# A linear-attention and gated feed-forward kernel: new load order, batch 0 reordered, attention of batch 2 moved into H1

## The chip, the cores and the metric

The kernel runs on one core of a Trainium2 chip. The metric is the device time of one execution in microseconds (us), here the median of several runs; a profile of one execution shows where its time goes. The engines are PE (TensorE, the matrix products; PEld is its weight load), DVE (VectorE), ACT (ScalarE), POOL (GpSimd) and SP (SyncE, which here only issues DMAs).

## The reference

Inputs q, k, v have 8 batches of 8 heads, 576 rows and 64 columns, in f32. The output has 4608 rows of 512.

```python
def phi(x):
    return np.where(x > 0, x, np.exp(x) - 1.0) + 1.0
q_p, k_p = (phi(q), phi(k))
kv = np.einsum('bhsd,bhse->bhde', k_p, v)
z = np.sum(k_p, axis=2)
num = np.einsum('bhsd,bhde->bhse', q_p, kv)
den = np.einsum('bhsd,bhd->bhs', q_p, z)[..., None] + 1e-06
attn = num / den                        # x: rows of 8 heads x 64 = 512
h = x @ w_in                            # 512 -> 2048
g = h * (1.0 / (1.0 + np.exp(-beta * h)))
y = g @ w_out                           # 2048 -> 512
```

## The kernel before

Each batch has two halves. The attention makes phi(q) and phi(k) in bf16 (ACT's exp, DVE's relu and min: `phi_part`, `phi_relu`, `phi_min`, lines 133 to 153), the products k'v with a column of ones that gives the sums of k (`kv_products`, `kv_both`, lines 169 to 192), the transposes of phi(q) (`q_trans` on PE, or `q_trans_dma`, a DMA transpose from SP), five blocks of numerators with a denominator, a reciprocal and a product on DVE each (`numer`, line 229), and the transposes of the result into `xT` (`x_trans` on PE, `x_trans_dma` from SP). The feed-forward part has an H phase, 16 groups `ff` of four products of 512 columns each with a silu on ACT, and a Y phase, four row blocks of 16 products, evicted by DVE and stored by SP in two DMAs each (`y_out`, line 307). The 576 rows of a batch are 512 plus 64; the eight remainders of 64 make a ninth feed-forward pass at the end, the tail.

The order is written out by hand (`tc.manual_schedule()`): each engine executes its instructions in the order of the program text, and SP and POOL are also the queues that DMAs are issued from. The order is:

- Loads (lines 90 to 111). Eight heads lie as four per half of the partitions, so `load` issues two DMAs of 64 partitions for each tensor (line 80). POOL issues the loads that turn f32 into bf16: half of k, half of q and v of batch 0, w_in in four parts, k and q of batch 1. SP issues the other halves of k and q of batch 0 in f32 (`k0f`, `q0f`), beta, later w_out and v.
- Batch 0 (lines 341 to 404): ten warm products, beta, phi k, six warm products, phi q, copies of v into `vaug`, k'v, the five numerators and transposes interleaved with the first four `ff`, then the rest of H0. w_out and v of batch 1 are issued from SP in it, k and q of batch 2 from POOL (line 405). DVE multiplies half of w_out by 1/beta, POOL the other half (`w_out_scale`).
- Y0 (lines 410 to 442): three quarters of the y products, then the attention of batch 1 between the last quarter's.
- H1 and Y1 (lines 475 to 492): H1 has loads and copies of v beside it; Y1 has the attention of batch 2, with transposes on PE.
- From batch 2 on (line 495) H of batch b holds the numerators of batch b+1 and Y its phi of batch b+2, with transposes by DMA.

PSUM has four banks for h and y (`mmps`), two for the numerators (one buffer, `numps`) and two for transposes and k'v (`miscps`). Output goes through three rotating `y_sb` buffers; e and r of phi have three each.

Of the kernel before, what the change touches and what calls it, by code (L numbers as in the profile page):

```python
# [16 lines left out]
def kernel(  # L17
# [21 lines left out]
    EA = D + 1  # L39
    TINY = 2.0 ** -30  # L40

# [3 lines left out]
    mmps = ctx.enter_context(tc.tile_pool(name="mmps", bufs=4, space=bass.MemoryType.PSUM))  # L45
    numps = ctx.enter_context(tc.tile_pool(name="numps", bufs=1, space=bass.MemoryType.PSUM))
    miscps = ctx.enter_context(tc.tile_pool(name="miscps", bufs=2, space=bass.MemoryType.PSUM))
    work = ctx.enter_context(tc.tile_pool(name="work", bufs=2))


    NX = 3
    xk = [consts.tile([P, 4, J, D], BF16, name=f"xk{i}") for i in range(NX)]
    xq = [consts.tile([P, 4, J, D], BF16, name=f"xq{i}") for i in range(NX)]
    vf = [consts.tile([P, 4, J, D], F32, name=f"vf{i}") for i in range(2)]
# [3 lines left out]
    xT = [consts.tile([P, KC, 512], BF16, name=f"xT{i}") for i in range(3)]  # L58
# [3 lines left out]
    warm = consts.tile([P, 512], BF16, name="warm")  # L62

# [5 lines left out]
    k0f = stage[:, 0:1152].rearrange("p (h j d) -> p h j d", h=2, j=J)  # L69
    q0f = stage[:, 1152:2304].rearrange("p (h j d) -> p h j d", h=2, j=J)  # L70
    v0b = vf[0].rearrange("p h j d -> p (h j d)").bitcast(BF16)[:, 0:2304].rearrange(
        "p (h j d) -> p h j d", h=4, j=J
    )

    def heads(src, b, hh, h0, n):
        return src[b, hh * 4 + h0 : hh * 4 + h0 + n].rearrange(
            "h (g j) d -> g h (j d)", j=J
        )

    def load(eng, dst, src, b, h0=0, n=4):  # L80
        return [
            eng.dma_start(  # L82
                out=dst[hh * G : (hh + 1) * G].rearrange("p h j d -> p h (j d)"),
                in_=heads(src, b, hh, h0, n),
            )
            for hh in range(2)
        ]
# [3 lines left out]
    load(nc.gpsimd, xk[0][:, 0:2], k, 0, 0, 2)  # L91
    load(nc.sync, k0f, k, 0, 2, 2)
    load(nc.gpsimd, xq[0][:, 0:2], q, 0, 0, 2)
    load(nc.sync, q0f, q, 0, 2, 2)
    beta_row = consts.tile([FC, P], F32)
    nc.sync.dma_start(out=beta_row, in_=moe_beta.rearrange("(c p) -> c p", p=P))
    load(nc.gpsimd, v0b[:, 0:2], v, 0, 0, 2)
# [8 lines left out]
    w_in_dma = [  # L106
        nc.gpsimd.dma_start(out=w_in_sb[i], in_=w_in_v[:, :, i * 512 : (i + 1) * 512])
        for i in range(4)
    ]
    load(nc.gpsimd, xk[1], k, 1)  # L110
    load(nc.gpsimd, xq[1], q, 1)

    def load_w_out(i, after=None):
        d = nc.sync.dma_start(out=w_out_f[i], in_=w_out_v[:, i * 4 : (i + 1) * 4, :])
        if after is not None:
            tc.add_manual_dep(d.ins, after.ins.name, SYNC, reason="share of the queues")
# [4 lines left out]
    nc.vector.memset(kvmask[D:P, :, 1, :], 1.0)  # L121
    for i in range(2):
        nc.vector.memset(vaug[i][:, :, :, :, D : D + 2], 1.0)

    def idle(n, cols=512):
        for _ in range(n):
            wp = mmps.tile([P, 512], F32, tag="mm", name="warm_ps")
            nc.tensor.matmul(wp[:, 0:cols], warm[:, 0:P], warm[:, 0:cols], start=True, stop=True)
# [4 lines left out]
    def phi_part(b, a, pr, x):  # L133

        e = work.tile([P, 2, J, D], BF16, tag="e", name="e", bufs=3)
        nc.scalar.activation(e, x, ACTF.Exp)  # L136
        st[b, a, pr, "e"] = e

    def phi_relu(b, a, pr, x):
        r = work.tile([P, 2, J, D], BF16, tag="r", name="r", bufs=3)  # L140
        nc.vector.tensor_scalar(r, x, 0.0, 1.0, ALU.max, ALU.add)  # L141
        st[b, a, pr, "r"] = r

    def phi_tile(b, a):
        st[b, a] = work.tile([P, 2, J, P], BF16, tag=f"phi{a}", name=f"phi_{a}")
# [9 lines left out]
    def xin(b, a, pr):  # L155
        if b == 0:
            if pr == 1:
                return k0f if a == "k" else q0f
            return (xk if a == "k" else xq)[0][:, 0:2]
        return (xk if a == "k" else xq)[b % NX][:, 2 * pr : 2 * pr + 2]  # L160

    def v_copy(eng, b, pr):
        src = v0b if b == 0 else vf[b % 2]
        eng.tensor_copy(  # L164
            vaug[b % 2][:, pr, :, :, 0:D],
            src[:, 2 * pr : 2 * pr + 2].rearrange("p h j d -> p j h d"),
        )

    def kv_products(b, prs, ps):
        for pr in prs:  # L170
            for j in range(J):
                for hh in range(2):
                    r = slice(hh * G, (hh + 1) * G)
                    nc.tensor.matmul(  # L174
                        ps[hh, pr],
                        st[b, "k"][r, pr, j, :],
                        vaug[b % 2][r, pr, j, :, 0:EA],
                        start=(j == 0), stop=(j == J - 1), skip_group_check=True,
                    )

    def kv_tile(b):
        st[b, "kv"] = work.tile([P, 2, 2, 2 * EA], BF16, tag="kv_bd", name="kv_bd")

    def kv_both(b):

        t = [miscps.tile([P, 2, 2 * EA], F32, tag="misc", name="kvp") for _ in range(2)]
        kv_products(b, (0, 1), {(hh, pr): t[hh][:, pr] for hh in range(2) for pr in range(2)})
        kv_tile(b)
        for hh in range(2):
            nc.vector.tensor_mul(  # L190
                st[b, "kv"][:, hh], t[hh], kvmask.rearrange("p a g e -> p a (g e)")
            )

    def q_trans(b, t, eng):

        js = [j for j in (2 * t, 2 * t + 1) if j < J]
        if t == 0:
            st[b, "qT"] = work.tile([P, NT, 2, 2, P], BF16, tag="qT", name="qT")
        tp = miscps.tile([P, 2, 2, 2, G], BF16, tag="misc", name="qtp")
        for pr in range(2):  # L200
            for i, j in enumerate(js):
                nc.tensor.matmul(  # L202
                    tp[:, pr, :, i, :], st[b, "q"][:, pr, j, :], identity,
                    is_transpose=True, start=True, stop=True, skip_group_check=True,
                )
        n = len(js) * G
        dst = st[b, "qT"][:, t, :, :, 0:n].rearrange("p a h n -> p (a h) n")
        src = tp.rearrange("p a h i g -> p (a h) (i g)")[:, :, 0:n]
# [4 lines left out]

    def q_trans_dma(b):
        st[b, "qTd"] = work.tile([P, 2, 2 * J, G], BF16, tag="qT", name="qTd")
        for hh in range(2):
            nc.sync.dma_start_transpose(
                out=st[b, "qTd"][:, hh],
                in_=st[b, "q"][hh * G : (hh + 1) * G].rearrange("p a j c -> p (a j c)"),
            )  # L220

    def q_stat(b, t, hh, pr, n):
# [4 lines left out]
        return st[b, "qT"][:, t, pr, hh, 0:n]  # L227

    def numer(b, t):
        n = P if t < NT - 1 else G  # L230
        nps = numps.tile([P, 2, 512], F32, tag="num", name="nps")
        for hh in range(2):
# [11 lines left out]
        xs = work.tile([P, 2, 4, D], BF16, tag="xs", name="xs", bufs=4)  # L244
        nc.vector.tensor_mul(  # L245
            xs[:n], nv[:, :, :, 0:D], rden[:n, :, :, None].to_broadcast([n, 2, 4, D])
        )
        st[b, "xs", t] = xs

    def x_dst(b, t):  # L250
        if t < NT - 1:
            return xT[b % 3][:, :, t * P : (t + 1) * P]
        return xT_tail[:, :, b * G : (b + 1) * G]

    def x_trans(b, t, eng):
        n = P if t < NT - 1 else G
        xv = st[b, "xs", t].rearrange("p a h d -> p (a h d)")
        tp = miscps.tile([P, KC, P], BF16, tag="misc", name="xtp")
        for p in range(KC):
            nc.tensor.matmul(  # L260
                tp[:, p, :n], xv[:n, p * P : (p + 1) * P], identity[:n, :n],
                is_transpose=True, start=True, stop=True, skip_group_check=True,
            )
        if eng is nc.scalar:
            nc.scalar.copy(x_dst(b, t), tp[:, :, :n])
        else:
            eng.tensor_copy(x_dst(b, t), tp[:, :, :n])

    def x_trans_dma(b, t):
        n = P if t < NT - 1 else G  # L270
        nc.sync.dma_start_transpose(
            out=x_dst(b, t),
            in_=st[b, "xs", t][:n].rearrange("p a h d -> p (a h d)"),
        )


    def h_mm(b, x, ff, hp, c0=0, c1=512):
# [13 lines left out]
    def mm_tile(name):  # L291
        return mmps.tile([P, 512], F32, tag="mm", name=name)

# [10 lines left out]
    def rows(b, j):  # L304
        return out[b * S : (b + 1) * S, :].rearrange("(g j) m -> j g m", j=J)[j]

    def y_out(b, t, yp, c0=0, c1=512, eng=None):
        y_sb = work.tile([P, DM], F32, tag="y_sb", name="y_sb", bufs=3)
        (eng or nc.vector).tensor_copy(y_sb[:, c0:c1], yp[:, c0:c1])  # L309
        for i in range(2):  # L310
            dst = rows(b, 2 * t + i) if b < B else rows(2 * t + i, J - 1)
            nc.sync.dma_start(out=dst[:, c0:c1], in_=y_sb[i * G : (i + 1) * G, c0:c1])

    def w_out_scale(eng, i):
        for c in range(4):
# [3 lines left out]
                None, ALU.mult,  # L319
            )  # L320

    def load_kq(b):
        if b < B:
            load(nc.gpsimd, xk[b % NX], k, b)
            load(nc.gpsimd, xq[b % NX], q, b)

    def load_v(b):
        if b < B:
            load(nc.sync, vf[b % 2], v, b)

    def phi_all(b, a):
        phi_tile(b, a)
        for pr in range(2):
            phi_part(b, a, pr, xin(b, a, pr))
        for pr in range(2):
            phi_relu(b, a, pr, xin(b, a, pr))
        for pr in range(2):
            phi_min(b, a, pr)


    idle(10)
    bps = miscps.tile([P, FC], F32, tag="misc", name="bps")
# [202 lines left out]
```

## Time and profile before

| | us |
|---|---|
| median of 3 runs (325.47 to 330.0) | 328.07 |
| the profiled execution, first to last instruction | 328.0 |
| busy: PE, ACT, DVE, POOL | 295.7, 160.2, 119.4, 55.6 |
| mean granted PE clock | 0.951 |

The profiled execution gives its span, first to last instruction; no other time of its own is listed for it. The page also divides the span into 40 slices (a digit is the busy share in tenths), and the trace gives, for any stretch, the busy time of each engine, the granted clock of PE (1.00 or 0.50) and what the DMAs moved, and for each instruction how long its engine was idle before it and what ended that. Waits and shares are inferred from semaphore events. Batches from the third on repeat with a period of 30.3 us.

### The profile page before, as it was taken

The numbers are of one execution on the slowest core, as the hardware profiler recorded it, in microseconds if no ns is written. First come the engines' busy times: TensorE is split into PE (matmuls) and PEld (weight loads), VectorE is DVE, ScalarE is ACT, GpSimd is POOL, SyncE is SP. The second block draws the span as 40 slices with busy tenths as digits, with TensorE's granted clock in tenths as the row PEclk, the third lists the DMA queues.
The fourth block names the chain that finished last, engine by engine and source line by source line (L and its number), as shares of the span: only waits on it lengthen the run. The fifth ranks groups of instructions, "written<-read, shape, count | busy, mean of one in ns | idle before, by whom it ended". The sixth has DMA issues, their size and how long they took to land.

```text
span 328.0 us, 4511 instructions
## 1 busy us (share of the span) xinstructions
PE 295.7 (90%) x1739; PEld 144.9 (44%) x1767; DVE 119.4 (36%) x272; ACT 160.2 (49%) x208; POOL 55.6 (17%) x70
## 2 busy tenths in 40 slices
PE   5377899786999499999999999999999999999994
PEld 1145544532455244445444544554454444444443
DVE  1564606351048905532551436154425110010011
ACT  0612885362692247816682585378256018306600
POOL 8520067940220004102300200020000000000000
PEclk9565999997899979999999999999999999999999
DMA  7999998299519187987988525942723140041032
GB/s 171 210 207 280 286 273 208 37 187 211 132 26 189 27 155 143 174 146 196 129 132 191 141 43 82 199 113 28 152 50 64 40 88 10 0 97 33 0 66 65
DMA packets 47510, 40.82 MB, mean 124 GB/s; under 512 B 26352, under 2 KB 36864, under 8 KB 47488
## 3 DMA queue, kind: packets, MB, share of 16 engines
q1 hardware_dynamic: 36608, 28.99, 40.3%
q0 software_dynamic: 10880, 11.54, 22.5%
q8 instruction: 14, 0.23, 0.3%
q14 instruction: 8, 0.07, 0.1%
HBM read 36.71 MB, written 9.44 MB: 141 GB/s over the span
## 4 chain that ended last, share of the span: by engine, by line
PE 82%; DVE 7%; DMA 4%; issue 3%; ACT 2%; SPq 1%; DVEq 0%
PE h_ps L279 38%; PE y_ps L297 36%; PE nps L234 4%; PE kvp L174 3%; DMA beta_row<-in_moe_beta_dram 2%; DVE xs L245 2%; DMA out_dram<-y_sb 2%; DVE y_sb L309 1%; PE qtp L202 1%; SPq L82 1%; DVE rden L243 1%; ACT qT L210 1%; DVE r L141 1%; DVE phi_q L148 1%; PE xtp L260 1%
## 5 line engine op out<-in xcount | busy, mean ns | idle before, releaser
L287 ACT ACTIVATE g<-h_ps,beta_c 128x512 bf16<-128x512 f32 x144 | 98.2, 687 | 105.5 <-PE h_ps L279 103.3
L279 PE MATMUL h_ps<-xT,w_in 128*128 128x512 bf16 (+1 forms) x513 | 122.8, 386 | 8.5 <-DVE y_sb L309 3.5
L297 PE MATMUL y_ps<-w_out,g 128*128 128x512 bf16 (+2 forms) x580 | 127.2, 374 | 1.3 <-DVE y_sb L309 0.6
L279 PEld LDWEIGHTS <-w_in 128*128 128x128 bf16 x592 | 57.5, 100 | 71.7 <-issue 13.9
L297 PEld LDWEIGHTS <-g 128*128 128x128 bf16 x592 | 57.0, 98 | 64.9 <-issue 0.8
L309 DVE COPY y_sb<-y_ps 128x512 f32<-128x512 f32 (+2 forms) x37 | 24.8, 673 | 88.0 <-PE y_ps L297 82.2
L164 POOL CAST vaug<-vf 128x1152 bf16<-128x1152 f32 x14 | 16.6, 1214 | 123.2 <-DMA vf<-in_v_dram 98.1
L245 DVE TENSOR_TENSOR xs<-nps,rden 128x512 bf16<-128x512 f32 (+1 forms) x40 | 27.6, 690 | 1.4
L148 DVE TENSOR_TENSOR phi_k<-e,r 128x1152 bf16<-128x1152 bf16 x16 | 12.1, 787 | 25.6 <-ACT e L136 25.6
L136 ACT ACTIVATE e<-xk 128x1152 bf16<-128x1152 bf16 x15 | 16.7, 1151 | 7.5 <-DVE phi_q L148 7.4
L242 DVE TENSOR_SCALAR den<-nps 128x8 f32<-128x8 f32 (+1 forms) x40 | 6.5, 164 | 32.0 <-PE nps L234 32.0
L148 DVE TENSOR_TENSOR phi_q<-e,r 128x1152 bf16<-128x1152 bf16 x16 | 11.8, 753 | 13.9 <-ACT e L136 13.9
L136 ACT ACTIVATE e<-xq 128x1152 bf16<-128x1152 bf16 x15 | 16.5, 1151 | 0.0
L317 POOL TENSOR_SCALAR w_out<-stage,rbeta 128x512 bf16<-128x512 f32 x8 | 12.6, 1591 | 20.8 <-DMA stage<-in_moe_w_out_dram 20.8
L190 DVE TENSOR_TENSOR kv_bd<-kvp,kvmask 128x260 bf16<-128x260 f32 x14 | 5.3, 423 | 26.9 <-PE kvp L174 26.9
L279 PE MATMUL h_ps<-xT_tail,w_in 128*128 128x512 bf16 x63 | 13.9, 379 | 0.1
L136 ACT ACT_TABLE_LOAD x7 | 9.0, 1283 | 8.9 <-DMA xk<-in_k_dram 8.8
L82 POOL DMA_DIRECT2D xk<-in_k_dram x16 | 10.2, 645 | 9.7 <-ACT e L136 5.3
L174 PE MATMUL kvp<-vaug,phi_k 64*128 64x130 bf16 x288 | 10.9, 229 | 0.4 <-ACT qT L210 0.3
L82 POOL DMA_DIRECT2D xq<-in_q_dram x16 | 10.4, 663 | 4.5 <-DMA w_in<-in_moe_w_in_dram 3.8
L174 PEld LDWEIGHTS <-phi_k 64*128 64x128 bf16 x288 | 9.3, 100 | 4.1 <-issue 2.6
L234 PEld LDWEIGHTS <-qTd 128*128 128x128 bf16 (+1 forms) x100 | 7.5, 100 | 6.8 <-DVE xs L245 2.1
(46 smaller groups left out, 116.1 us busy)
## 6 DMA issues: line engine op xcount, KB each, us to landing
out_dram<-y_sb SPq DMA_DIRECT2D x70, 128.0 KB, 2.4
vf<-in_v_dram SPq DMA_DIRECT2D x14, 576.0 KB, 7.3
xk<-in_k_dram POOLq DMA_DIRECT2D x14, 288.0 KB, 6.6
xq<-in_q_dram POOLq DMA_DIRECT2D x14, 288.0 KB, 9.6
w_in<-in_moe_w_in_dram POOLq DMA_DIRECT2D x4, 512.0 KB, 10.6
g<-in_moe_w_out_dram SPq DMA_DIRECT2D x2, 1024.0 KB, 13.1
stage<-in_moe_w_out_dram SPq DMA_DIRECT2D x2, 1024.0 KB, 22.5
stage<-in_k_dram SPq DMA_DIRECT2D x2, 288.0 KB, 4.3
```

What stands on the lines that cost most here:

```text
L82: eng.dma_start(out=dst[hh * G : (hh + 1) * G].rearrange("p h j d -> p h (j d)"), in_=heads(src, b, hh, h0, n),)
L136: nc.scalar.activation(e, x, ACTF.Exp)
L148: nc.vector.tensor_tensor(st[b, a][:, pr].rearrange("p j (h d) -> p j h d", h=2), st[b, a, pr, "e"].rearrange("p h j d -> p j h d"), st[b, ...
L164: eng.tensor_copy(vaug[b % 2][:, pr, :, :, 0:D], src[:, 2 * pr : 2 * pr + 2].rearrange("p h j d -> p j h d"),)
L174: nc.tensor.matmul(ps[hh, pr], st[b, "k"][r, pr, j, :], vaug[b % 2][r, pr, j, :, 0:EA], start=(j == 0), stop=(j == J - 1), skip_group_chec ...
L234: nc.tensor.matmul(nps[:n, hh, pr * 2 * EA : (pr + 1) * 2 * EA], q_stat(b, t, hh, pr, n), st[b, "kv"][:, hh, pr, :], start=True, stop=True ...
L245: nc.vector.tensor_mul(xs[:n], nv[:, :, :, 0:D], rden[:n, :, :, None].to_broadcast([n, 2, 4, D]))
L279: nc.tensor.matmul(hp[:, c0:c1], w_in_sb[ff // 4][:, kc, (ff % 4) * P : (ff % 4 + 1) * P], x[:, kc, c0:c1], start=(kc == 0), stop=(kc == K ...
L287: nc.scalar.activation(g_sb[b % 2][:, ff, :], hp, ACTF.Silu, scale=beta_c[:, ff : ff + 1])
L297: nc.tensor.matmul(yp[:, c0:c1], g_sb[b % 2][:, ff, t * P : (t + 1) * P], w_out_sb[i][:, c, c0:c1], start=(ff == 0), stop=(ff == FC - 1), ...
L309: (eng or nc.vector).tensor_copy(y_sb[:, c0:c1], yp[:, c0:c1])
L317: eng.tensor_scalar(w_out_sb[i][:, c, :], w_out_f[i][:, c, :], rbeta[:, ff : ff + 1], None, ALU.mult,)
```

## The change

- Loads: head 2i+a takes the partition half a, so one DMA of 128 partitions brings a tensor. SP issues only the first half of q and beta. All else goes on POOL in the order q, k, v of batch 0, w_in, half of w_out, k, q, v of batch 1, the other half of w_out, k and q of batch 2, and so on. k and q have two buffers instead of three, v one.
- Batch 0: a dummy exp at the start, q before k, one product column for the sums of k and a set of 20 two-column products for all denominators ahead of the second half of v, then the numerators without denominators; the first four `ff` in passes of 128 columns.
- PSUM: four single banks and two pairs; k'v, numerators and transposes share the pairs. Transposes of q go 1024 columns at a time.
- Y0: the third quarter of y moves behind the attention products; the first y block is evicted by ACT, the exps of batch 2 start there. Two tiles with four fixed slots replace `y_sb`. `w_out_scale` multiplies by 1/beta and by 1.0.
- H1 holds the numerators of batch 2, as later H phases do for theirs; Y1 becomes like the later Y phases. e and r of phi have two buffers, phi q and phi k one.
- `FAST` is empty: `y_fast`, `w_sums`, `g_diff` and `g_sums` issue nothing.

The core of the diff:

```diff
+    q0f = stage[:, 2048:3200].rearrange("p (i j d) -> p i j d", i=2, j=J)
+    def load(eng, dst, src, b, i0=0, n=4):
+        return eng.dma_start(
+            out=dst.rearrange("p i j d -> p i (j d)"),
+            in_=src[b].rearrange("(i a) (g j) d -> (a g) i (j d)", a=2, j=J)[:, i0 : i0 + n],
         )
-    load(nc.gpsimd, xk[0][:, 0:2], k, 0, 0, 2)
-    load(nc.sync, k0f, k, 0, 2, 2)
-    load(nc.gpsimd, xq[0][:, 0:2], q, 0, 0, 2)
-    load(nc.sync, q0f, q, 0, 2, 2)
+    nc.scalar.activation(act0, warm[:, 0:1], ACTF.Exp)
+    load(nc.sync, q0f, q, 0, 0, 2)
...
+    load(nc.gpsimd, xq[0][:, 2:4], q, 0, 2, 2)
+    load(nc.gpsimd, xk[0][:, 0:2], k, 0, 0, 2)
+    load(nc.gpsimd, xk[0][:, 2:4], k, 0, 2, 2)
     load(nc.gpsimd, v0b[:, 0:2], v, 0, 0, 2)
     load(nc.gpsimd, v0b[:, 2:4], v, 0, 2, 2)
...
+    def load_w_out(i):
+        nc.gpsimd.dma_start(out=w_out_f[i], in_=w_out_v[:, i * 4 : (i + 1) * 4, :])
+    load_w_out(0)
+    load_w_out(1)
     load(nc.gpsimd, xk[1], k, 1)
     load(nc.gpsimd, xq[1], q, 1)
...
+    idle(6)
...
+    phi_part(0, "q", 0)
+    phi_part(0, "q", 1)
+    q_trans(0, (0,), (nc.vector,))
+    phi_part(0, "k", 0)
+    q_trans(0, (1,), (nc.scalar,), nc.vector)
+    phi_part(0, "k", 1)
+    for pr in range(2):
+        for j in range(J):
+            for hh in range(2):
+                nc.tensor.matmul(
+                    zps[:, hh, pr : pr + 1], st[0, "k"][half(hh), pr, j, :], ones[half(hh)],
...
+    kv_first(0)
+    for t in range(NT):
+        n = rows_of(t)
+        for hh in range(2):
+            for pr in range(2):
+                nc.tensor.matmul(
+                    dps[:n, t, hh, pr], st[0, "qT"][:, pr, t, hh, 0:n], zbd[:, hh, pr, :],
...
+    idle(3)
+    kv_first(1)
+    for t in range(4):
+        numer_first(t, bank("nps0", [P, 2, 2, P]))
...
+    for t in range(4):
+        x_trans(0, t, nc.scalar, xtp0[:, t % 2, t // 2])
+        if t:
+            for ff in range(4):
+                h_mm(xT[0], ff, hp0[ff], (t - 1) * P, t * P)
...
+    load_v(1)
     load_w_out(2)
-    load_v(1)
     load_w_out(3)
+    load_kq(2)
...
+    for pr in range(2):
+        v_copy(nc.gpsimd, 1, pr)
+    load_v(2)
+    for i in range(2):
         for t in range(4):
             y_mm(0, t, i, yps[t])
+    w_out_scale(nc.gpsimd, 2)
     w_out_scale(nc.gpsimd, 3)
+    q_trans(1, (0, 1), (nc.scalar, nc.vector), nc.vector)
     kv_both(1)
+    for t in range(2):
+        y_mm(0, t, 2, yps[t])
     numer(1, 0)
...
+    y_out(0, 0, yps[0], eng=nc.scalar)
+    phi_exp(2, "k", 0, xin(2, "k", 0))
     y_mm(0, 2, 3, yps[2])
+    x_trans(1, 4, nc.vector)
+    y_out(0, 1, yps[1])
+    phi_exp(2, "k", 1, xin(2, "k", 1))
     y_mm(0, 3, 3, yps[3])
+    y_out(0, 2, yps[2])
+    y_out(0, 3, yps[3])
+    for pr in range(2):
+        phi_relu(2, "k", pr, xin(2, "k", pr))
+        phi_min(2, "k", pr)
+    for pr in range(2):
+        phi_part(2, "q", pr)
+    load_kq(3)
...
+    for b in range(1, B + 1):
+        n, m = b + 1, b + 2
...
+            if n == 2:
+                at(sh, 0, lambda: q_trans_dma(2))
+                at(sh, 0, lambda: [v_copy(nc.gpsimd, 2, pr) for pr in range(2)], lambda: load_v(3))
             at(sh, 3, lambda: kv_both(n))
             for t in range(NT):
-                at(sh, 5 + 2 * t, lambda t=t: numer(n, t))
-                at(sh, 6 + 2 * t, lambda t=t: x_trans_dma(n, t))
+                at(sh, (6, 8, 9, 10, 12)[t], lambda t=t: numer(n, t))
+                at(sh, (6, 8, 9, 10, 12)[t], lambda t=t: x_trans_dma(n, t))
+        if m < B:
+            at(sy, y(0, 0), lambda: phi_tile(m, "q"), lambda: phi_part(m, "q", 0))
+            at(sy, y(1, 0), lambda: phi_part(m, "q", 1))
+            at(sy, y(3, 2), lambda: q_trans_dma(m))
+            at(sy, y(6, 2), lambda: phi_all(m, "k"))
+            at(sy, y(6, 4), lambda: [v_copy(nc.gpsimd, m, pr) for pr in range(2)])
+            at(sy, y(7, 5), lambda: load_kq(m + 1), lambda: load_v(m + 1))
```

Here `y(a, f)` gives `a`. `phi_part` of the new kernel is exp, relu and min of one half; `kv_first` is 18 products of k'v without the column of ones, and one product with the mask; `numer_first` is four products and one product on DVE with the reciprocals made earlier.

## The prediction

> **What bounds the kernel now.** I read the page's 40 slices first, then the busy time by stage, then the timeline around every place where TensorE (PE) idles, then the clock by 3.4 us stretches. The slices:
>
> ```profile
> PE   5377899786999499999999999999999999999994
> PEclk9565999997899979999999999999999999999999
> ```
>
> From slice 15 (115 us) on PE is full at full clock; before that it is neither. By stage (stretch, length, busy time and count of PE, PEld, DVE, ACT, POOL, granted clock, DMA share, GB/s):
>
> ```profile
> 0.00:36.80 36.80, 22.17 (x147) 12.74 (x148) 17.14 (x46) 11.77 (x16) 13.86 (x28) 0.72 1.09 224
> 36.80:47.20 10.40, 10.32 (x48) 4.70 (x49) 2.41 (x6) 8.99 (x14) 3.12 (x3) 1.00 1.11 277
> 47.20:70.50 23.30, 19.90 (x157) 10.45 (x157) 11.77 (x25) 11.40 (x17) 19.71 (x18) 1.00 0.75 150
> 70.50:90.60 20.10, 16.73 (x62) 6.92 (x65) 2.59 (x5) 11.55 (x17) 2.23 (x2) 0.83 0.81 169
> 90.60:114.60 24.00, 19.16 (x157) 10.52 (x158) 18.95 (x45) 11.96 (x12) 2.60 (x4) 1.00 0.44 83
> 114.60:146.70 32.10, 31.71 (x181) 15.11 (x185) 12.45 (x29) 17.89 (x22) 4.95 (x6) 0.95 0.90 154
> 146.70:177.00 30.30, 30.14 (x183) 14.59 (x184) 12.95 (x29) 17.88 (x22) 4.63 (x6) 1.00 0.91 154
> ```
>
> The rows are: start, rest of H0, Y0 with attention of batch 1, H1, Y1 with attention of batch 2, then whole batches. A batch in the steady state is 30.3 us with PE busy for 30.1: nothing is left there without fewer products. Y alone is 64 products of 512 columns, 64 x 0.216 = 13.8 us (the chain has 7.12 + 6.64), so H with attention is 16.5. The early stages hold what can be had: Y1 takes 24.0 instead of 13.8, H1 20.1, the next batch 32.1 instead of 30.3, and the start. Where PE stands there (start, us, engine, line, operation, idle before it and who ended it):
>
> ```profile
> 8.80 1.28 ACT L136 ACT_TABLE_LOAD   x1 [8.80 <-DMA xk<-in_k_dram]
> ...
> 44.08 6.19 POOL L317 TENSOR_SCALAR w_out<-stage,rbeta 128x512 bf16<-128x512 f32 x4 [19.18 <-DMA stage<-in_moe_w_out_dram]
> ...
> 77.51 0.69 DVE L309 COPY y_sb<-y_ps 128x512 f32<-128x512 f32 x1 [5.85 <-DMA out_dram<-y_sb]
> ...
> 78.25 12.54 PE L279 MATMUL h_ps<-xT,w_in 128*128 128x512 bf16 x43 [3.24 <-DVE y_sb L309]
> ```
>
> The first exp waits for k and then for a table load; at 77.5 DVE waits for an output DMA to give a y_sb buffer back, and PE with it. That stall is paid twice, as the clock shows:
>
> ```profile
> 19.30:22.70 3.40, 3.40 (x41) 2.19 (x40) 1.87 (x5) 0.00 (x0) 1.17 (x2) 0.50 1.24 206
> 22.70:26.10 3.40, 1.65 (x22) 1.17 (x20) 1.72 (x7) 1.40 (x4) 0.61 (x1) 1.00 1.19 230
> ...
> 73.90:77.30 3.40, 1.11 (x6) 0.39 (x4) 0.00 (x0) 1.49 (x3) 0.00 (x0) 1.00 1.14 245
> 77.30:80.70 3.40, 2.45 (x6) 0.84 (x6) 1.43 (x3) 0.55 (x1) 0.00 (x0) 0.50 0.86 226
> 80.70:84.10 3.40, 3.40 (x9) 1.18 (x8) 0.00 (x0) 1.36 (x3) 0.00 (x0) 0.50 0.89 188
> ```
>
> A stretch in which PE is full is followed by clock 1.00, one in which it is half idle or more by 0.50; the two half-clock stretches after the stall cost 3.4 us.
>
> **The change, stage by stage.** The sum is made against the profiled span, 328.0 us; the median of the three runs is 328.07, so I take them as the same.
>
> *Start to the end of H0 (47.2 before).* Loads: the first half of q goes alone on SP (one call for two); k's first half on SP took 4.3 us to land from issues at 0.73 and 1.56, so q lands at about 6.1. The other five half tensors go on POOL's queue at 206 GB/s of landed bytes (0.295 MB in 1.4 us each): q 7.5, k 8.4 and 9.8, v 11.3 and 12.7, then w_in 2.5 each, the last at 23. The dummy exp takes the 1.28 us table load off the path, so the first exp runs at 6.1 instead of 10.1. Then ACT and DVE alternate: exp 1.15, relu 0.4 to 0.95, min 0.75, one 1024-wide copy of qT on each engine (twice 0.42, twice 0.58, wider than any row). Both phis are done at about 14.0; before, the last min ended at 17.95. After that PE is in order. Sums of k: of 36 one-column products, 18 lie behind the last min; the kvp products at half clock took 2.06 for 36, so 1.0 (to 15.1, two small copies beside). kv first half 1.0 (16.1). Twenty two-column denominator products: no row; between 0.03 each (kvp, full clock, 1.16 for 36) and 0.155 (nps at half clock, 0.62 for 4), I take 0.10, nps at full clock: 2.0 (18.1). Three warm products 0.43 each: 1.3 (19.4). kv second half 1.0 or, at full clock, 0.6 and its mask product 0.49: 20.9. Numerator 0.4, xs 0.69 (den and reciprocal are gone from here: 5 x 0.37 saved), transposes 0.4, copy 0.58: first h at 23.2. Four passes of 16 products of 128 columns: 0.11 at half clock, 0.055 at full, with transposes 0.4 each and a short wait for the last xs: 5.8, half of it at half clock, to 29.0. Before, this point was 36.8. Twelve h groups of 0.866 follow: H0 ends at 39.4, **-7.8**. Ends: dps and h all at full clock 36.5; all at half clock and loads 1 us later 43.
>
> *Y0 with attention of batch 1 (23.3 before).* 32 y products 6.9 (46.3). ACT reaches table load and four exps after the last silu (40.3 + 1.3 + 4.6 = 46.2), min q 47.0, transposes to 47.8, copies on ACT then DVE (1.05 + 0.8, in series by the order's waits), kv 1.2: 50.2. Then eight y groups of 0.866 and, between them, five numerators (0.42) and transposes (0.4): 11.0, to 61.2. So 21.8: **-1.5**. POOL must keep up: the w_out loads and v now follow in its queue, and no f32 load on POOL is in the trace. Bounds: the 206 GB/s of its casting loads, and SP's w_out rate, 281 GB/s with peaks over 400 between 47 and 52. I take 350, since the bytes and the tile shape are SP's: w_out0 26, w_out1 29, k 32, q 35, v 38.5, w_out2 and 3 by 42 and 45. Then POOL: casts of v 3.1 (41.6), scaling 6.2 and 6.4 as before (48.5, 55), needed at 50.2 and 55.9. It fits, by 1 us. The second multiplication in the scaling has no POOL row; on DVE the two-op relu costs 0.65 ns an element against 0.9 for the one-op scaling, so zero; the upper end is double, 12.6 more in all.
>
> *H1 with attention of batch 2.* PE work as in the steady state, 16.5. Four separate y slots instead of three rotating ones remove the 5.85 us DMA wait. What is late next: DVE must copy y (0.9), do both phi k (2 x 1.15) after Y0; with two e buffers instead of three, exp q waits for these mins, its second ends 4.4 after Y0, the table load 1.28 comes behind it, and the first silu ends at 6.4. PE has four PSUM banks and kv until then, 4.65: **wait 1.8**. Then phi q ends at 5.5, the two DMA transposes of q take 1.9 of SP each and land 4.4 after issue (SP rows of qTd), so at 11.8; PE wants the first numerator at 9.0: **wait 2.8**. Queued behind them on SP are the xT transposes, which have a whole Y of room. Half clock after these waits: none to 3.4, partly absorbed by the second wait; I take 0.9. H1 22.0 against 20.1: **+1.9**, between -3.6 (no wait) and +6.
>
> *Y1*: 13.8 against 24.0: **-10.2**. *Batch 2*: no half clock, 30.3 against 32.1: **-1.8**. *The rest* (181.3): same products. The numerators at slots 8, 9, 10 come every 1.1 us and DVE needs 1.06 for each; two PSUM buffers cover that. v, k and q loads are issued in Y, half a batch ahead, though v has one buffer now: 0.
>
> Sum: 328.0 - 7.8 - 1.5 + 1.9 - 10.2 - 1.8 = 308.6, say **309**.
>
> **Weighed against the Trainium skill.** POOL's 36 load issues took 0.61 to 0.77 us each, among them four at 12.4 to 15.0 with DVE in relu and min, so I charge the moved issues nothing. The page "SBUF — State Buffer", section "SBUF: two separate sides", speaks against the move: while DVE runs a two-port operation, GpSimd cannot write descriptors, and an issue of 620 ns becomes 3100. By that, the eleven w_out and v issues moved from SP could cost up to 2.5 us each of POOL time, an estimate of 27 us, some 10 of them ahead of Y0's scaling, and the sum would be about 319.
>
> **Rivals.**
> 1. POOL becomes the bound of Y0. For: 19.7 of 23.3 us busy there already, 1 us of slack by my count. At 206 GB/s for f32, 5.1 us for each w_out and 5.7 for v, w_out3 lands 10 us later and scaling ends at 62.5, 6.6 after PE's need: 315. With a doubled scaling cost alone it ends at 67: 320; with both, at 75: 328.
> 2. The start gains only half: the chain to the first h is the same length in instructions, and its PE work sits at half clock, as 9.0 to 22.7 and 26.1 to 32.9 before. H0 ends at 43: 313.
> 3. H1 has no waits (exps early enough): 303.
> 4. Slower: the single load queue starves the steady state. One v buffer and 2.4 MB landing through POOL per batch; q of the next batch would hold PE. Against: loads have from the middle of Y to the end of the next H, 22 us, and need 9 to 10. It decides when a batch's loads take over 22 us: to lose 19 us, six batches must each lose 3.2, so loads of 25 us; for +2% 26.3. At 30 us a load: 309 + 6 x 8 = 357.
> 5. The change doesn't do what it says: the q-first order gains nothing because all queues share the DMA engines. The order alone puts q ahead, so only part: this is inside rival 2.
>
> **How the numbers follow.** Forecast 309 (range of its own 304 to 314) 0.60; rival 1 0.13; rival 2 0.10; rival 3 0.08; rival 4 0.04; a mixture of 1 and 2, or both halves of 1, 322 to 328, 0.05. The range 302 to 320 leaves out rival 4, the mixture and a tail of rival 3: under 2 in 10. About 2% (321.5 and 334.6) is what a measurement of this kernel can tell from no change: faster 0.91, same 0.05 (the mixture), slower 0.04.
>
> **What would show it.** First exp near 6; first h near 23 and the last of H0 near 39.4; POOL's last w_out scaling ending before PE asks for it (about 55); H1 starting near 61 with two PE waits, one on ACT's silu, one on a DMA of qTd; Y1 of 13.8 and batches of 30.3. I am wrong if PE waits for POOL in Y0, if batches exceed 30.5, or if the clock stays at 0.5 through H0.

## The result: slower, and the profile after

The changed kernel takes 337.97 us (median of 4 runs, 337.09 to 339.54) beside 328.72 us (325.47 to 330.0) for the kernel before on the same chip: a ratio of 1.029, 95% interval 1.023 to 1.035. The forecast was 309. The profiled execution took 338.02 us, with a span of 336.1.

From the page, the slices of PE and of its granted clock:

```profile
PE   4487997971999899969999399999999999999994
PEclk9998799976799999996999699999999999999999
```

The early dip of the clock in before (slices 2 to 4) is gone. But PE now drops in slices 9 and 10, 18 and 23, that is in H1, H3 and H4, and the clock drops in these or the next ones (9 to 11, 19, 23). By stage (start, length, busy time and count of PE, PEld, DVE, ACT, POOL, granted clock, DMA share, GB/s), for the end of H0, Y0, H1, Y1, H2, then H3, H4 and the batch after it:

```profile
22.90:43.70 20.80, 18.02 (x129) 9.62 (x127) 5.51 (x15) 12.90 (x19) 7.04 (x9) 0.84 1.10 327
43.70:64.90 21.20, 18.95 (x158) 10.26 (x157) 11.57 (x28) 10.81 (x13) 9.80 (x12) 1.00 0.87 204
64.90:95.50 30.60, 21.59 (x123) 9.80 (x122) 12.67 (x29) 15.09 (x20) 4.49 (x6) 0.78 0.72 151
95.50:109.30 13.80, 13.80 (x65) 6.23 (x64) 6.03 (x10) 7.64 (x7) 2.24 (x3) 1.00 0.59 79
109.30:126.90 17.60, 16.69 (x122) 8.33 (x120) 7.04 (x19) 10.31 (x15) 2.24 (x2) 1.00 0.82 197
...
140.50:163.80 23.30, 19.50 (x122) 9.34 (x121) 7.07 (x19) 10.31 (x16) 2.24 (x2) 0.85 0.68 158
...
177.60:201.80 24.20, 18.78 (x121) 9.08 (x120) 7.07 (x19) 10.31 (x15) 2.24 (x2) 0.86 0.76 156
201.80:232.10 30.30, 30.30 (x185) 14.57 (x184) 13.06 (x29) 17.95 (x22) 0.00 (x0) 1.00 0.40 74
```

| stage | predicted | measured |
|---|---|---|
| start to end of H0 | 39.4 | 43.7 |
| Y0 with attention of batch 1 | 21.8 | 21.2 |
| H1 with attention of batch 2 | 22.0 | 30.6 |
| Y1 | 13.8 | 13.8 |
| H2, H3, H4 | 3 x 16.5 | 17.6, 23.3, 24.2 |

The gaps are +4.3, -0.6, +8.6, 0 and +15.6; together 27.9, against 27.5 between the span and the sum of the forecast. From H5 on, when the last loads are over, nothing is lost: the batch at 201.8 is 30.3 again. What PE waits for (us in total, times, longest), and how long the transposes of q took from issue to landing in 95 to 200 us:

```profile
PE nps L266 <- DMA qTd<-phi_q: 16.9, 5, 6.3
PE h_ps L302 <- ACT g L310: 5.0, 3, 2.2
```

```profile
DMA to landing us min/median/max: 4.0/9.9/17.8
```

The same line of before (115 to 240 us):

```profile
DMA to landing us min/median/max: 3.9/4.8/5.4
```

The chain of work that ended last now holds four of these landings (start, us), on which H1, H2, H3 and H4 wait; its DMA share is 19%, against 4% before:

```profile
74.00 9.61 DMA qTd<-phi_q
...
105.46 12.14 DMA qTd<-phi_q
...
135.31 16.55 DMA qTd<-phi_q
...
172.58 17.78 DMA qTd<-phi_q
```

The timeline (start, us, engine, line, operation, idle before and who ended it) shows two places, the middle of H0 and the passage from Y2 to H3:

```profile
30.30 2.91 PE L302 MATMUL h_ps<-xT,w_in 128*128 128x512 bf16 x8 [2.01 <-ACT g L310]
33.99 9.82 PE L302 MATMUL h_ps<-xT,w_in 128*128 128x512 bf16 x36 [0.78 <-ACT g L310]
...
133.92 3.78 SPq L241 DMA_TRANSPOSE qTd<-phi_q  x2
134.83 0.75 POOL L90 DMA_DIRECT2D xk<-in_k_dram  x1 [15.25 <-issue]
135.57 0.76 POOL L90 DMA_DIRECT2D xq<-in_q_dram  x1
136.30 0.78 POOL L90 DMA_DIRECT2D vf<-in_v_dram  x1
137.79 4.75 SPq L334 DMA_DIRECT2D out_dram<-y  x6
...
151.91 0.40 PE L266 MATMUL nps<-kv_bd,qTd 128*128 128x130 bf16 x2 [3.80 <-DMA qTd<-phi_q]
```

The reader is to see that three loads, 2.3 MB as they land, are issued within 2.4 us of the first transpose of q, and that the numerator at 151.9 waits for the second. The moment is set by buffers: with two for k, the load may start when the phi of the batch that held the buffer has been read, which is in the middle of Y (DVE's last relu of k ends at 134.3 here), just when the transposes start. Before, with three, POOL issued these loads in H (129.98 and 155.9 us), beside the transposes `xT`, which have a whole Y to land; when the transposes of q were issued there, at most the tail of one load was still moving (up to 139 us).

### The profile page after: what moved, and what is told of

Its sections match the earlier page's. It is cut to its first block, busy times and chain, and to the rows that moved or that the text cites. A ratio compares the mean times of both kernels' runs of the same rounds, so it can differ in the third digit from the quotient of the medians.

```text
span 336.1 us, 4543 instructions
## 1 busy us (share of the span) xinstructions
PE 297.6 (89%) x1806; PEld 145.0 (43%) x1806; DVE 115.6 (34%) x259; ACT 158.8 (47%) x202; POOL 48.7 (14%) x64
## 4 chain that ended last, share of the span: by engine, by line
PE 62%; DMA 19%; DVE 7%; ACT 6%; SPq 3%; issue 3%; DVEq 0%; ACTq 0%; POOLq 0%
PE h_ps L302 32%; PE y_ps L317 22%; DMA qTd<-phi_q 17%; PE nps L266 3%; SPq L241 2%; ACT e L144 2%; DVE phi_q L156 2%; DMA xq<-in_q_dram 2%; DVE r L149 2%; ACT L144 2%; DVE y L214 1%; ACT g L310 1%; DVE phi_k L156 1%; PE kvp L193 1%; PE xtp L290 1%
## 5 line engine op out<-in xcount | busy, mean ns | idle before, releaser
L302 PE MATMUL h_ps<-xT,w_in 128*128 128x512 bf16 (+1 forms) x560 | 129.9, 384 | 5.0 <-ACT g L310 5.0
L302 PEld LDWEIGHTS <-w_in 128*128 128x128 bf16 x624 | 59.4, 102 | 71.0 <-issue 17.8
L214 DVE COPY y<-y_ps 128x512 f32<-128x512 f32 (+2 forms) x36 | 24.1, 674 | 84.7 <-PE y_ps L317 84.7
L266 PE MATMUL nps<-kv_bd,qTd 128*128 128x130 bf16 (+1 forms) x120 | 13.9, 237 | 16.9 <-DMA qTd<-phi_q 16.9
L276 DVE TENSOR_TENSOR xs<-nps,rden 128x512 bf16<-128x512 f32 (+1 forms) x35 | 24.1, 689 | 1.4 <-DVE rden L275 0.2
L266 PEld LDWEIGHTS <-qTd 128*128 128x128 bf16 (+1 forms) x120 | 9.7, 107 | 27.4 <-DMA qTd<-phi_q 18.2
L144 ACT ACTIVATE e<-xk 128x1152 bf16<-128x1152 bf16 x16 | 18.1, 1158 | 0.4 <-DMA xk<-in_k_dram 0.4
L90 POOL DMA_DIRECT2D xk<-in_k_dram x9 | 7.0, 774 | 59.8 <-issue 51.5
L212 ACT COPY xT<-xtp 128x512 bf16<-128x512 bf16 x8 | 4.7, 585 | 18.2 <-PE xtp L290 18.2
L193 PE MATMUL kvp<-vaug,phi_k 64*128 64x130 bf16 x252 | 8.6, 217 | 1.7 <-DVE qT L214 1.7
L193 PEld LDWEIGHTS <-phi_k 64*128 64x128 bf16 x252 | 7.3, 94 | 4.4 <-issue 2.5
```

The source lines that it names most:

```text
L90: return eng.dma_start(out=dst.rearrange("p i j d -> p i (j d)"), in_=src[b].rearrange("(i a) (g j) d -> (a g) i (j d)", a=2, j=J)[:, i0 : ...
L193: nc.tensor.matmul(t[:, hh, pr * 2 * EA : (pr + 1) * 2 * EA], st[b, "k"][half(hh), pr, j, :], vaug[b % 2][half(hh), pr, j, :, 0:EA], start ...
L214: eng.tensor_copy(dst, src)
L266: nc.tensor.matmul(nps[:n, hh, pr * 2 * EA : (pr + 1) * 2 * EA], q_stat(b, t, hh, pr, n), st[b, "kv"][:, hh, pr, :], start=True, stop=True ...
L276: nc.vector.tensor_mul(xs_tile(b, t), nv[:, :, :, 0:D], rden[:n, :, :, None].to_broadcast([n, 2, 4, D]))
L302: nc.tensor.matmul(hp[:, c0:c1], w_in_sb[ff // 4][:, kc, (ff % 4) * P : (ff % 4 + 1) * P], x[:, kc, c0:c1], start=(kc == 0), stop=(kc == K ...
```

## The experiments

The theory (A): the loads take the DMA engines from the transposes of q, and the half clock after PE's waits adds to what it loses. The rivals: the transposes are late because they are issued later in Y than before (B), and the pairs of PSUM banks or other waits in H0 and H1 carry the loss (C).

**Loads held until the transposes have landed.** The changed kernel with one dependency:

```diff
-            nc.sync.dma_start_transpose(
+            st[b, "qTi"] = nc.sync.dma_start_transpose(
...
-            load(nc.gpsimd, xk[b % 2], k, b)
+            d = load(nc.gpsimd, xk[b % 2], k, b)
+            if (b - 2, "qTi") in st:
+                tc.add_manual_dep(d.ins, st[b - 2, "qTi"].ins.name, SYNC, reason="transposes first")
```

> The changed kernel with one edit: from batch 4 on, the k, q and v loads of a batch wait until the DMA transposes of q that are issued at the same time have landed. Theory A (the loads, issued from POOL as soon as phi has freed its buffer, share the DMA engines with the q transposes and stretch their landing from 4 to 5 us to 10 to 18): qTd lands in 4 to 6 us, PE's 16.9 us of waits on qTd fall to 3 or less (H1 only), H3 and H4 come to 16.5 to 17 each instead of 23.3 and 24.2 with no half clock; span near 313, time near 315. Rival B (the transposes are late by themselves: issued behind two stores, one buffer for phi q and its transposes): qTd waits stay, time 336 to 340. Rival C (without the head start the loads of the next batch come late): ACT waits for q at the start of Y, batches over 31.

Measured: 314.09 us (313.23 to 315.11), ratio to before 0.959 (0.953 to 0.964). H1 and H2, the landings over the whole run, and what PE waits for them (16.9 us in the changed kernel):

```profile
64.70:86.05 21.35, 18.14 (x122) 8.76 (x121) 11.01 (x27) 14.69 (x20) 2.25 (x3) 0.92 0.79 137
...
99.90:116.30 16.40, 16.40 (x121) 8.30 (x120) 7.77 (x19) 10.25 (x15) 4.74 (x5) 1.00 1.11 211
```

```profile
DMA to landing us min/median/max: 4.0/4.3/5.7
```

```profile
PE nps L266 <- DMA qTd<-phi_q: 1.0, 1, 1.0
```

The same bytes, the same single queue and the same buffers, moved by some microseconds: H1 is 21.35 and H2 16.4, where 22.0 and 16.5 were forecast. The loss of 24 us was the overlap of these transfers.

**Three buffers for k and q**, as the kernel before had (`range(2)` to `range(3)`, `b % 2` to `b % 3`):

> The changed kernel with three buffers for k and for q, as before the change. Theory A: POOL then issues the loads in H, a batch earlier, when the v copy is done, away from the q transposes; qTd lands in 4 to 6 us in the steady state, H3 and H4 16.5 to 17, time near 315 (H1 may keep a part, since the loads of batch 4 start near 65 and last 9 us): 314 to 320. Rival B: qTd waits stay, 336 to 340.

Measured: 319.86 us (319.6 to 321.03), ratio 0.977 (0.971 to 0.983). The landings over the whole run are 3.9/4.5/7.7, and none over 5.3 from 95 us on; PE waits 3.7 us for `qTd`, both times in H1 (27.1 us long), and not after. So the buffer was what put the loads beside the transposes from H2 on; in H1 loads still run there.

**Transposes of q one slot earlier**, at `y(2, 2)` instead of `y(3, 2)`, without the dependency:

> The changed kernel with only the q transposes issued one slot earlier in Y, ahead of the two stores of the first y block, as before the change. Rival B (they are late because they are issued behind the stores and the loads start first): issue comes about 1.9 us earlier, most of a landing is over before the loads start, waits on qTd fall from 16.9 to 4 or less, time 314 to 322. Theory A (sharing with the loads from 1 us after the issue on is what stretches them): landing still 8 to 16, waits fall by about 2 us in each of three batches, time 328 to 334.

Measured: 324.01 us (322.93 to 325.41, 10 runs), ratio 0.991 (0.988 to 0.995), between the two. The stages show why:

```profile
65.20:95.90 30.70, 20.79 (x120) 9.62 (x121) 12.45 (x29) 14.88 (x20) 4.47 (x5) 0.78 0.74 149
...
109.70:126.10 16.40, 16.20 (x119) 8.30 (x120) 7.04 (x19) 10.24 (x15) 2.24 (x2) 1.00 0.90 214
```

H1, whose transposes are issued at its head and not in Y, is as slow as in the changed kernel; H2 loses nothing. The transposes now start 2.7 us ahead of the first load (101.3 and 104.0) instead of 0.9. That head start is enough, so B is right that the place in Y counts, and A that it counts only because of the loads.

**The loads in thirds.** In the changed kernel each steady load of k and q becomes three calls, pieces of 384 B instead of 1152 B, same bytes and place:

```diff
-            load(nc.gpsimd, xk[b % 2], k, b)
-            load(nc.gpsimd, xq[b % 2], q, b)
+            for x, src in ((xk, k), (xq, q)):
+                for j in range(0, J, 3):
+                    nc.gpsimd.dma_start(
+                        out=x[b % 2][:, :, j : j + 3].rearrange("p i j d -> p i (j d)"),
...
```

> The changed kernel with one edit: each steady load of k and of q (128 partitions, pieces of 1152 B per packet in the trace) is issued as three calls, so that its pieces are 384 B; same bytes, same place in the order. Theory A1 (the transposes of q are slow beside the loads because the DMA engines take one packet of each queue in turn; alone some 764 transpose packets of 256 B pass in 1.5 us, beside the loads 210): a load packet of a third of the bytes holds the engine for a shorter time, so more transpose packets pass, qTd lands 7 to 11 us after issue at the worst instead of 17.8, and the time falls from 338.0 to between 322 and 332. Rival A2 (the engines share by bytes, or the transposes stand behind the whole load, so packet size does not matter): landings to 14 to 18 us and 335 to 341 us. POOL issues four more calls of about 0.75 us for each batch, which nothing waits for.

Measured: 330.01 us (327.87 to 332.02, 10 runs), ratio 1.004 (1.000 to 1.007), in A1's range. Landings in 95 to 200 us: 3.9/7.6/11.1. Packets that start in a stretch of 1.5 us, counted from the trace, in the same passage from Y2 to H3; the stretches beside the loads are those with both kinds moving throughout (140.75 to 145.5 for k and q and 146.5 to 148.5 for v in the changed kernel, 146.75 to 151.25 in thirds):

| load beside the transposes | transposes alone, 256 B | transposes beside the load | the load's packets then |
|---|---|---|---|
| k, q in pieces of 1152 B | up to 863 | 209 to 223 | 205 to 213 |
| v in pieces of 4608 B | | 121 to 125 | 116 to 124 |
| k, q in pieces of 384 B | up to 895 | 277 to 467 | 358 to 446 |

The counts of the two kinds stay near each other, though the sizes differ 4.5 and 18 times, which fits engines that take a packet of one queue, then of the other; the counts don't show the order itself. The Trainium skill has this rule: "DMA: Bandwidth & Descriptors", section "Queues, rings and completion order", says that each DMA engine goes round its queues packet by packet. A transpose of 256 B packets beside packets of 1152 B then keeps a quarter of its rate (some 215 of 863), as the counts show. H2 and H3 became 16.5 each. H1, however, took 35.5 us, with a landing of 16.7, which lies outside A1's 7 to 11; why this one became worse is not settled.

**The same overlap in the kernel before.** Loads of k and q of batches from 5 on are held to the transposes' moment, and v moves to POOL beside them:

```diff
-            load(nc.gpsimd, xk[b % NX], k, b)
+            d = load(nc.gpsimd, xk[b % NX], k, b)
+            if b >= 5:
+                tc.add_manual_dep(d[0].ins, st[b - 1, "q", "min"].ins.name, SYNC, reason="beside the transposes")
...
-            load(nc.sync, vf[b % 2], v, b)
+            load(nc.gpsimd if b >= 5 else nc.sync, vf[b % 2], v, b)
```

> The kernel before with the suspected cost planted: from batch 5 on the loads of k, q and v of a batch are all issued from POOL together with the DMA transposes of q of the batch before it. Theory A: those qTd transposes land in 10 to 18 us instead of 4 to 5.4; PE has some 15 us before it needs them, so it waits 0 to 4 us in up to three batches and runs at half clock after the longer waits: 330 to 342. Rival B: landing unchanged, time as before, 327 to 330.

Measured: 365.01 us (361.54 to 365.92), ratio 1.112 (1.104 to 1.120), more than expected. Landings reach 18.7 us, but PE does not wait for them first:

```profile
PE h_ps L279 <- DVE y_sb L309: 34.0, 5, 10.1
```

The stores of y are queued behind the slow transposes on SP, and the three `y_sb` buffers do not come free: in one Y the stores are issued from 139.3 us on, but their packets move only from 149.5 on, when those of the transposes end. The overlap is harmful there too, through another victim. In the changed kernel PE waits 0.6 us for y in all, though its stores took 12.8 us (median) to land in 120 to 155 us; it has four slots, two in each of two tiles.

**Products of a pair ahead of its silus.** For `ff` 4 to 7 of H0 each pair of PSUM banks is filled and emptied half by half. Here both halves' products stand ahead of both silus:

```diff
     for ff in range(4, 8, 2):
         hp = banks("h_ps")
         for i in range(2):
             h_mm(xT[0], ff + i, hp[:, i])
+        for i in range(2):
             silu(0, ff + i, hp[:, i])
```

> The changed kernel with one edit in H0: in groups 4 to 7, both products of a PSUM pair stand ahead of the pair's two silus. Theory A2 (the product of the second half of a pair waits for the silu of the first half, since the pair is one tile): the PE waits of 2.0 and 0.8 us on ACT near 28 and 33 go, and the two half-clock stretches behind them (3.4 us lost), H0 ends near 38 instead of 43.7; time 331 to 333. Rival (the silu table load at 26 us is what is late): PE waits in the same place a little later, time 336 to 338.

Measured: 336.3 us (333.6 to 339.07), ratio 1.0235 (1.016 to 1.031). H0 is cured, the total is not:

```profile
22.90:39.80 16.90, 16.57 (x129) 10.75 (x129) 5.05 (x14) 12.73 (x20) 3.25 (x4) 1.00 1.09 336
```

H0 ends at 39.8, 0.4 from the forecast, at full clock. Most of the 3.9 us is given back: PE waits 1.8 us for phi q in Y0, and for `qTd` 18.1 us in all instead of 16.9. C holds for H0 alone.

**Both mends together** (the dependency and the pairs):

> Both edits together: loads after the q transposes, and the products of groups 4 to 7 ahead of their silus. The first alone measured 314.09, the second alone 336.3 against 337.97. Theory: H0 ends near 39.8 instead of 43.4, but Y0 then waits for ACT's exps and gives 1 to 2 us back; 310.5 to 312.5. Rival (all of it is given back, since ACT's chain from the last silu to phi q sets Y0): 313.5 to 315.

Measured: 311.77 us (310.85 to 315.12, 6 runs), ratio 0.958 (0.951 to 0.964). The profiled span is 308.9; H0 ends at 37.6 there, and Y0 takes 24.2 instead of the 21.5 of the hold alone.

**Three buffers each for e and r** on top (`bufs=3`), so that exp q need not wait for the mins:

> As the run beside it, with three buffers for e and for r instead of two. Theory (two e buffers make exp q of batch 2 wait for the mins of k, so the first silu of H1 comes 1 to 2 us late): PE's wait of 2.2 us on ACT at the start of H1 shrinks to under 1 us, time 1 to 2 us under the run beside it. Rival (DVE's chain of mins sets phi q, its transposes and so the first numerator of batch 2, whatever ACT does): the wait moves to qTd, time within 0.7 us.

Measured: 313.71 us (312.45 to 315.85), ratio 0.961 (0.955 to 0.967). No gain: PE's waits for silu fall from 2.5 to 1.3 us, and others rise in their place (`qTd` 1.7 instead of 0.9, phi k 0.9).

**Transposes at slot 2** on top of both mends:

> The best version so far (loads held until the transposes, products of a pair ahead of its silus: 311.8 us) with the transposes of q issued one slot earlier in Y. If the hold alone cures the late landings, the slot is worth nothing more: PE waits for qTd 0 to 1 us in all, 310.5 to 312.5. Rival: the transposes now stand ahead of two stores on SP and start the loads 1.9 us earlier, beside nothing: gain of the last 0.9 us wait in H1, 309.5 to 311, or, if the stores come late and hold y, 313 or more.

Measured: 313.71 us (310.64 to 315.18, 6 runs), ratio 0.951 (0.946 to 0.956): not told apart from 311.77. PE waits 2.2 us for `qTd` in the profiled execution, more than the 0 to 1 that was expected. No gain of the slot shows beside the hold.

**Without the dummy exp** on top of both mends:

> The best version so far (311.8 us) without the dummy exp at the start. The prediction counted the 1.28 us of the table load as path. If so: 313.1. Rival: the second exp waits for its own data (the second half of q, 1.95 us idle before it), so a first exp that comes 1.3 us later still ends ahead of that, and only its relu, min and transposes move, which are one step before those of the second half: 311.5 to 312.3.

Measured: 311.53 us (310.02 to 315.65, 6 runs), ratio 0.947 (0.943 to 0.952). From ACT's timeline, this kernel:

```profile
0.72 1.28 ACT L144 ACT_TABLE_LOAD   x1 [0.72 <-PEq L688]
4.17 1.16 ACT L144 ACTIVATE e<-stage 128x1152 bf16<-128x1152 f32 x1 [2.17 <-DMA stage<-in_q_dram]
6.87 1.16 ACT L144 ACTIVATE e<-xq 128x1152 bf16<-128x1152 bf16 x1 [1.54 <-DMA xq<-in_q_dram]
```

The table load starts at 0.72 without the dummy too. Neither view had it: in before it stood behind the wait for k, here it does not. With the dummy the first exp starts at 4.41 (both mends), without it at 4.17: no gain of the dummy shows.

**Scaling with one operation.** The hold alone, and `w_out_scale` without the second multiplication:

```diff
-                1.0, ALU.mult, ALU.mult,
+                None, ALU.mult,
```

> Loads after the transposes, and the scaling of w_out with one multiplication as before the change. Theory (the second multiplication picks a quicker form on POOL: 0.68 us each now, 1.59 before): POOL's eight scalings take 12.5 us instead of 5.4, end near 54, before PE asks for w_out3 near 60; time within 1 us of 314.1. Rival (the w_out tiles are quicker for another reason, such as the buffers): 0.68 stays. Rival for time (POOL becomes the bound of Y0): 317 or more.

Measured: 317.64 us (316.16 to 321.77), ratio 0.971 (0.963 to 0.979), against 314.09 and 0.959 for the hold alone. The profiled execution is the slowest of the four; the others took 316.16 to 318.78. POOL's scaling, first with the hold alone, then with one operation (ns least, median, most; first and last start):

```profile
L342 POOL TENSOR_SCALAR w_out<-stage,rbeta x8: 681/682/701, 40.8 to 45.5; 128x512 bf16<-128x512 f32 x8
```

```profile
L342 POOL TENSOR_SCALAR w_out<-stage,rbeta x8: 1552/1554/1751, 41.4 to 52.4; 128x512 bf16<-128x512 f32 x8
```

The scaling still ends at 54.2, ahead of the y products that need it (59.9). In this execution the loss in Y0 comes through DVE, whose mins of phi run beside it; from DVE's timelines, again in that order:

```profile
46.57 0.76 DVE L156 TENSOR_TENSOR phi_k<-e,r 128x1152 bf16<-128x1152 bf16 x1 [14.57 <-ACT e L144]
47.24 0.45 DVE L149 TENSOR_SCALAR r<-xk 128x1152 bf16<-128x1152 bf16 x1
```

```profile
48.75 1.68 DVE L156 TENSOR_TENSOR phi_k<-e,r 128x1152 bf16<-128x1152 bf16 x1 [16.43 <-ACT e L144]
50.35 0.66 DVE L149 TENSOR_SCALAR r<-xk 128x1152 bf16<-128x1152 bf16 x1
51.11 1.05 DVE L156 TENSOR_TENSOR phi_k<-e,r 128x1152 bf16<-128x1152 bf16 x1
```

PE then waits 2.4 us for phi q, and its clock falls to 0.50 from 56.4 to 63.2: Y0 takes 26.1 instead of 21.5. H0 ends 2.2 us later as well, with 6.8 us of half clock in it instead of 3.4, and H1 takes 23.0 instead of 21.35; no cause was found for either. This execution lost 8.5 us of span, the other three some 2 to 5 us of time, so how much of theirs came through DVE is not shown.

**Loads in halves of 64 partitions**, on the hold alone: every load of q, k and v becomes two calls, one per half, as before the change.

> The version with the load of k held until the transposes (314.1 us) with one edit: every load of q, k and v is issued as two calls of 64 partitions each, as the kernel before did, on the same queue and in the same order. If the single 128-partition call is worth something by itself: twice the issues of about 0.75 us on POOL's queue at the start (five more there), so the later loads of batch 0 and w_in come 2 to 4 us later, and the time is 316 to 319. If only the order of the loads counts and the issues hide behind the transfers (a load of 1152 KB takes 12 us to land, its issue 0.75): 313 to 315.5.

Measured: 319.49 us (318.15 to 321.19), ratio 0.9715 (0.967 to 0.976); 5.4 us above the hold alone, and just above the range of the first view. Up to the end of H0 the DMAs move 231 GB/s instead of 256, though in the first 22 us the rates are the same (184 and 185). v of batch 1 is cast at 43.8 instead of 37.5, so the scaling runs from 47.6 to 55.8, over the mins, as in the experiment before: Y0 takes 25.9. H0 ends 1.9 us later and H1 takes 23.1. Whether the calls or the halves make the loads slower is not told apart.

## Why the prediction was wrong

The failed step is the last term of the sum, "The rest (181.3): same products", and in it "v, k and q loads are issued in Y, half a batch ahead, though v has one buffer now: 0". The prediction asked only whether the loads themselves would be late. They were not. Their price fell on what ran beside them: the transposes of q, for which the prediction kept the 4.4 us to landing of the rows of before, where no load ran beside them. That one figure was used in H1 (+8.6) and silently in H2 to H4 (+15.6), and the hold takes back nearly all of both.

- *Start to H0's end, 39.4, measured 43.7.* The first h was right (23.2, measured 22.9), by a shorter and a longer part: the first exp ran at 4.5 and not at 6.1, but the second waited for q. The miss is "Twelve h groups of 0.866 follow". The pairs of PSUM banks added two waits, 2.0 and 0.8 us, and PE then ran at half clock from 31.0 to 37.8. The second half's products waited for the silu of the first, as the experiment with the pairs shows; that order was in the kernel. Rival 2's number came true by another mechanism.
- *Y0, 21.8, measured 21.2.* Right. Rival 1 fell: the scaling was done at 46.5, not 55, each step 0.68 us instead of the 1.59 of before, and the loads came earlier. POOL's issues beside DVE's work took 0.74 to 1.02 us each in Y0, so the Trainium skill's warning (page "SBUF — State Buffer", section "SBUF: two separate sides") did not decide here. Its 620 and 3100 ns are times of a whole DMA issued from GpSimd; the prediction read them as times of an issue.
- *H1, 22.0, measured 30.6.* The wait for silu was 2.25 us (1.8 predicted). The wait for `qTd` was 6.3 and 0.5 (2.8 predicted), from a landing 11.0 us after issue, and some 14 us of half clock stood around it (72.0 to 75.4, 78.8 to 89.0) where 0.9 us was charged. With the hold H1 is 21.35.
- *Y1 and batch 2.* Y1 is 13.8, as predicted: the attention of batch 2 no longer stands in it. Batch 2 is 31.2 (30.3 predicted).
- *Rival 4* named the right queue and the right sign, but a victim that was not hit, q of the next batch, and so a threshold (loads over 22 us) that was not reached: the slowest landing in 120 to 155 us was v's 15.8.
- *Slips in the working.* The terms after min q in Y0 add up to 50.9, not 50.2. The sum is one of spans, and a time lies some 1.9 us above its span (338.02 beside 336.1), so the median of 328.07 was not the time of the span of 328.0. One of POOL's 36 load issues in before took 0.97 us, not 0.77 at most. At slice 15 of before the clock is still 0.7; it is full from slice 16 on. PE is busy for 2.45 of the 3.4 us at half clock after 77.3, so that stall cost less than 3.4 us of clock.

The version with both mends bears out the terms of H1 (21.8), Y1 (13.8) and the H after it (16.4). Its span of 308.9 beside the sum of 308.6 is partly luck: H0 there is 1.8 shorter and Y0 2.4 longer than forecast, and this execution was the fastest of its six.

## What to carry to other kernels

When loads change their place in the order, list what else is in flight at the new place, and give each of those transfers a new duration, since the rows of the old trace hold only for its own neighbours. A buffer fewer changes when a load starts, not only whether it is in time: find the instruction that frees the buffer, and see what stands there. Small-packet transfers on which an engine waits, such as transposes, go ahead of bulk loads by an explicit dependency or a head start; here 2.7 us was enough in Y, and 0.9 was not.

## What the runs showed of the hardware

- Packets of two queues move in nearly equal numbers, whatever their sizes: transposes of 256 B fell from up to 863 packets in 1.5 us to some 215 beside packets of 1152 B, to some 123 beside packets of 4608 B, and to 277 to 467 beside packets of 384 B.
- A POOL `tensor_scalar` of 128x512, f32 to bf16, takes 0.68 us with two operations and 1.55 with one (1.59 in before). What makes the longer form faster is not known.
- DVE's min with two inputs in SBUF takes 0.76 us alone and 1.05 to 1.68 beside POOL's scaling with one operation. The Trainium skill, "SBUF — State Buffer", section "Who interferes with whom", names this pair as one that contends, and calls the contention an exclusive lock. The trace does not show the second one waiting for the first one's end: the min from 51.11 to 52.16 lies inside one scaling step (50.68 to 52.43). The ends of POOL's instructions are rough in a profile, though.
